# Seven-product MLP sums kept in PSUM by bank-to-bank copies, residual rows parked in DRAM

## The chip, the cores and the metric

The kernel runs on one core of one Trainium2 chip. The metric is the device time of one execution in microseconds (us). The median of three runs before the change is 256.88 us (256.54 to 257.63). One execution of the same program was also taken by the hardware profiler. It is the source of every line quoted here.

The engines have their usual short names. PE is the matrix engine; PEld is its weight load. DVE is the vector engine, ACT the scalar engine, POOL the GpSimd engine, SP the sync engine. PE writes only PSUM, eight banks of 128 partitions by 512 float32. ACT and DVE read PSUM and write either memory. DMA queues are fed from POOL and from SP.

## The reference, cut to what matters

```
P = sort_net; five times: softmax over rows, then divide by column sums      (4, 8, 8, 8)
k_sorted, v_sorted = P applied to the 8 blocks of 96 tokens of k and v
attn = softmax(0.125 * q_block @ k_sorted_block^T) @ v_sorted_block          per block
x = attn, heads side by side                                                 (4, 768, 512)
u = x + real(FFT over tokens and channels of x)
un = (u - mean(u)) / sqrt(var(u) + 1e-6)                                     over channels
out = u + relu(un @ w_ch1) @ w_ch2              w_ch1 (512, 2048), w_ch2 (2048, 512)
```

There are 4 batches (b = 0 to 3) of 768 tokens, 8 heads of 64 channels, float32 in and out. The kernel computes matrix products in float16 with float32 sums.

## The kernel before, in words

**Tiles.** A batch is 6 tiles of 128 tokens (T = 0 to 5), in two groups g = 0 and 1 of three tiles (384 tokens). For T = 0 to 2 the rows of a tile are stored with plain DMAs from SP; for T = 3 to 5 the rows are in reversed token order and are written with an indirect DMA from POOL that takes the row numbers from the tile `rows`.

**Stages of a batch.** `kqt` mixes k with the sort matrix and transposes q; `scores` makes the products and exponentials; `av` makes the 8 products with v and a division; `dft1` and `dft2` make the Fourier part and leave u (tile `u`, a pool of six buffers; batch 2 has six others, `ux`), its mean and variance, the normalised rows `un` and their transpose `ut`. Then come the MLP's two products, `ff1` (hidden rows in `hr`) and `ff2`.

**The MLP.** Batch 0 uses plain products (`ff1`, `mlp`): for each of 16 hidden chunks and each group, 4 matmuls of 128x128 by 384 (L1558), one relu out of PSUM, then `ff2` with 16 matmuls of 512 columns (L1615) and one DVE sum with u (L1622).

From batch 1 on, `ff2` is a two by two block product done with seven block products instead of eight (Winograd's form of Strassen's method). The blocks are two groups of tokens, two halves of the hidden rows and two halves of the output. The weight sums T1, T2, T4 and t3 are made once (`w2_sums`); the sums of the hidden rows (S1, S2, S3, S4) are made per chunk by DVE (L1770). A chunk (`ff2_chunk`) is tile t of both groups. Its seven products (L1794, 8 matmuls of 256 columns each) go to four PSUM banks R1, Q, R6 and R7. The sums of products that the method needs are made by DVE, reading a bank and a tile in SBUF and writing SBUF (L1811, seven instructions per chunk), after one ACT copy of R1 (L1825). The sums end in u0 and u1, the residual tiles, and `store` writes these.

`ff1` uses seven products for batches 2 and 3 alone (`SEVEN = (2, 3)`, `ff1_seven`, L1694). A `pair(i)` is one of eight hidden chunk pairs: seven products of two matmuls of 384 columns in three banks A, D, Q. A is copied three times to SBUF by ACT while it grows (`snap`, L1714). DVE adds a copy to D or Q (L1702) and makes the relu in SBUF (L1708); one relu is made by ACT out of PSUM (L1732). The weight sums G1 to G4 are made once (`w1_sums`), with one of them written over a half of w1; the sums of normalised rows (E1, E2, E4) per batch by DVE (L1682).

**Order.** Nothing is scheduled at run time. Each operation is added to a `Plan` with the engines that may do it. Five lists written out in the source (`ORDER`) give the operations of PE, ACT, DVE, POOL and SP in the order in which each engine runs them, and so also which of ACT and DVE does an operation that both may do. The plan places tiles and PSUM banks in buffers by its own running estimate of times, and fills PE's early waits with dummy matmuls (L1973). The engines wait for each other by semaphores, each strictly in its list's order.

**Memory that is reused.** `kq` has eight slots of k and q: batch 0 and 2 use slots 0 to 3, batch 3 uses 4 to 7. T1, T2, T4 lie over slots 0 to 3, G1, G2, G4 over 4 to 7.

Of the kernel before, what the change touches and what calls it, by code (L numbers as in the profile page):

```python
# [32 lines left out]
SEVEN = (2, 3)  # L33
ORDER = {
# [32 lines left out]
    ),  # L67
    "ACT": (
# [1937 lines left out]
```

## Time and profile before

| | before |
|---|---|
| median of three runs | 256.88 us |
| span of the profiled execution, first to last instruction | 254.8 us |
| PE busy | 245.2 us |
| DVE busy | 234.2 us |
| ACT busy | 165.3 us |
| POOL busy | 57.5 us |
| mean granted TensorE clock | 0.997 |
| DMA from POOL / from SP | 18.35 MB / 7.71 MB |

The profiled execution's own time is not reported beside its span. The median of the runs is 2.1 us above the span, and this document takes these 2.1 us for what lies around the span. "Busy" is the time in which at least one instruction of the engine was under way. Instructions on one engine overlap by some tens of nanoseconds, so that an engine that shows as fully busy may still take more work. Idle time of an engine that nobody waits for costs nothing. In the tables of groups, a row has the source line, the engine, the operation, what it writes and reads, the shape, the count, then total busy us and mean ns of one.

### The profile page before, as it was taken

To read this page: it belongs to the slowest core of one execution; us is meant where nothing else is said; L and a number is where in the kernel's file an instruction comes from. 1 tells how busy PE (TensorE), PEld (TensorE's weight loads), DVE (VectorE), ACT (ScalarE), POOL (GpSimd) and SP (SyncE) were. 2 spreads that over 40 slices of the span, in tenths; PEclk is the share of its full clock that TensorE was granted. 3 is DMA by queue.
4 is the path that set the end of the run, shared out by engine and by line. 5 is a ranking of instruction groups with operands and counts; after the bars stand their busy time and mean duration, and the time that the engine had idled before them with its cause. 6 is when DMAs were issued, how large, how long until landed. Compare 5 with 4: busy or idle time off the path is not lost.

```text
span 254.8 us, 7461 instructions
## 1 busy us (share of the span) xinstructions
PE 245.2 (96%) x2996; PEld 167.0 (66%) x2996; DVE 234.2 (92%) x597; ACT 165.3 (65%) x376; POOL 57.5 (23%) x88
## 2 busy tenths in 40 slices
PE   4999999999999999999999999999999999999992
PEld 1347875566566676644667757888657887567882
DVE  4799998999999989978999998999999999999993
ACT  2599998999968879956797377622687323773000
POOL 8974532234400770003100000210100000050013
PEclk9999999999999999999999999999999999999998
DMA  6999999999942699524132002530202400220025
GB/s 134 202 215 300 210 217 214 208 211 187 150 49 75 86 193 120 64 43 136 44 38 44 1 8 46 98 125 35 82 3 41 84 3 0 85 88 37 3 82 207
DMA packets 42809, 26.54 MB, mean 104 GB/s; under 512 B 30234, under 2 KB 39208, under 8 KB 42772
## 3 DMA queue, kind: packets, MB, share of 16 engines
q0 software_dynamic: 23664, 18.35, 42.9%
q1 hardware_dynamic: 19110, 7.71, 15.0%
q8 instruction: 23, 0.38, 0.6%
q14 instruction: 12, 0.10, 0.1%
HBM read 29.07 MB, written 6.29 MB: 139 GB/s over the span
## 4 chain that ended last, share of the span: by engine, by line
PE 71%; issue 9%; DVE 9%; ACT 8%; POOL 2%; DMA 1%; POOLq 0%; DVEq 0%
PE bank L1558 15%; PE bank L1794 14%; PE bank L1694 12%; PE bank L1615 9%; PE bank L1275 4%; PE bank L1440 3%; PE bank L945 2%; PE bank L1236 2%; ACT vcx L855 2%; PE bank L1349 2%; POOL out_dram L1593 2%; DVE rt L1292 1%; PE bank L1444 1%; PE bank L1047 1%; PE bank L1140 1%
## 5 line engine op out<-in xcount | busy, mean ns | idle before, releaser
L1558 PE MATMUL bank<-ut,w1sb 128*128 128x384 f16 x256 | 48.2, 326 | 0.0
L1714 ACT COPY vsf<-bank 128x384 f32<-128x384 f32 x48 | 21.6, 482 | 24.0 <-PE bank L1694 23.6
L1245 ACT ACTIVATE ex<-bank 96x384 f32<-96x384 f32 x64 | 29.3, 487 | 7.6 <-PE bank L1236 6.2
L1558 PEld LDWEIGHTS <-w1sb 128*128 128x128 f16 x256 | 23.1, 98 | 14.1 <-issue 0.3
L1570 ACT ACTIVATE hr<-bank 128x384 f16<-128x384 f32 x56 | 26.3, 491 | 8.5 <-PE bank L1558 8.5
L1593 POOL DMA_INDIRECT out_dram<-u,rows x9 | 9.4, 1042 | 97.4 <-DVE u L1811 72.5
L1794 PEld LDWEIGHTS <-hr 128*128 128x128 f16 x288 | 28.2, 98 | 4.6
L1702 DVE TENSOR_TENSOR hr<-bank,vsf 128x384 f16<-128x384 f32 x48 | 25.2, 548 | 1.6 <-PE bank L1694 1.0
L1615 PE MATMUL bank<-w2sb,hr 128*128 128x512 f16 x96 | 23.6, 380 | 0.0
L1794 PEld LDWEIGHTS <-vcx 128*128 128x128 f16 x216 | 21.1, 98 | 3.2
L1694 PE MATMUL bank<-ut,w1sb 128*128 128x384 f16 x96 | 20.7, 326 | 0.0
L1794 PE MATMUL bank<-w2sb,hr 128*128 128x256 f16 x144 | 18.7, 272 | 0.0
L1275 PEld LDWEIGHTS <-eb 97*128 97x128 f16 x416 | 15.7, 98 | 3.1 <-issue 0.4
L1794 PE MATMUL bank<-kq,vcx 128*128 128x256 f16 x144 | 17.5, 272 | 0.0
L1694 PEld LDWEIGHTS <-w1sb 128*128 128x128 f16 x128 | 12.5, 98 | 7.5
L612 POOL DMA_DIRECT2D kq<-in_q_dram x18 | 15.4, 866 | 8.8 <-PE bank L1558 4.2
L1292 DVE TENSOR_TENSOR rt<-bank,rz 128x384 f16<-128x384 f32 x32 | 16.9, 547 | 0.2
L1275 PE MATMUL bank<-vsf,eb 97*128 97x65 f16 x416 | 16.9, 193 | 0.0
L855 ACT CAST ks<-bank 128x384 f16<-128x384 f32 x27 | 14.4, 555 | 3.1 <-PE bank L1140 3.0
L1260 ACT ACTIVATE eb<-ex,negone 96x384 f16<-96x384 f32 x26 | 15.9, 616 | 0.1
L855 ACT CAST vsf<-bank 96x512 f16<-96x512 f32 x22 | 14.2, 679 | 1.4 <-PE bank L945 1.4
L1258 DVE TENSOR_SCALAR eb<-ex 96x384 f16<-96x384 f32 x38 | 13.9, 371 | 0.6 <-ACT ex L1245 0.4
(195 smaller groups left out, 535.5 us busy)
## 6 DMA issues: line engine op xcount, KB each, us to landing
w1sb<-in_moe_w_ch_dram POOLq DMA_DIRECT2D x4, 512.0 KB, 18.6
w2sb<-in_moe_w_ch_dram POOLq DMA_DIRECT2D x4, 512.0 KB, 21.5
hr<-in_v_dram POOLq DMA_DIRECT2D x2, 768.0 KB, 8.8
kq<-in_v_dram POOLq DMA_DIRECT2D x2, 768.0 KB, 12.7
kq<-in_k_dram POOLq DMA_DIRECT2D x8, 192.0 KB, 6.5
kq<-in_q_dram POOLq DMA_DIRECT2D x16, 96.0 KB, 6.7
out_dram<-u SPq DMA_DIRECT2D x5, 256.0 KB
kq<-in_k_dram POOLq DMA_DIRECT2D x2, 384.0 KB, 11.7
```

The lines of the kernel that those rows point to most:

```text
L855: (nc.scalar.copy if e == "ACT" else V.tensor_copy)(dst, src)
L1245: nc.scalar.activation(ex.ap[0:96], pss[h2].ap[0:96, 0:384], AF.Exp, scale=SCALE),
L1260: nc.scalar.activation(ed, src, AF.Identity, bias=negone[0:96])
L1275: nc.tensor.matmul(po.ap[:, 65 * T:65 * T + 65], eb.ap[:, e0:e0 + 128], vsf[0:97, vi:vi + 65], start=(n == 0), stop=(n == len(WIN[T]) - 1) ...
L1292: P.add({"DVE": (0.465, 0.56)}, lambda _: V.tensor_tensor(rt.ap[:, :, D * h:D * h + D], po3()[:, :, 0:D], rz.ap[:, :, None].broadcast_to([ ...
L1558: nc.tensor.matmul(ps.ap[:, 0:GT], w1sb[:, c, 128 * fc:128 * fc + 128], ut.ap[:, c, :], start=(c == 0), stop=(c == 3))
L1570: nc.scalar.activation(hr[g][:, fc, :], ps.ap[:, 0:GT], AF.Relu)
L1615: nc.tensor.matmul(ps.ap, hr[g][:, fc, 128 * tt:128 * tt + 128], w2sb[:, fc, :], start=(fc == 0), stop=(fc == 15))
L1694: nc.tensor.matmul(ps.ap[:, 0:GT], lhs[:, c, fi], rhs()[:, c, :], start=(start and c == 0), stop=(c == 1), skip_group_check=True)
L1702: return P.add({"DVE": (0.47, 0.57)}, lambda _: V.tensor_tensor(hr[g][:, fc, :], p.ap[:, 0:GT], o.ap, op=ALU.add), r=r, w=hk(g, fc, fc + 1 ...
L1714: P.add({"ACT": act(GT)}, lambda _: nc.scalar.copy(x.ap, A.ap[:, 0:GT]), r=[A], w=[x], prio=pr_v - 1, tag="pc", after=avs)
L1794: nc.tensor.matmul(ps.ap[:, o:o + 256], lhs()[:, fc], rhs[:, fc], start=(start and fc == 0), stop=(fc == 7), skip_group_check=True)
```

## The change

1. `SEVEN` becomes (1, 2, 3): batch 1's first product is divided into seven as well. Its sums E and its copies use tiles of the pool `s`.
2. In `ff1_seven` a pair has two banks A and Q instead of three. Sums of products are made by copying one bank over another (`seed`, PSUM to PSUM, by ACT or DVE) and letting the next matmuls accumulate on the copy. One product (G3 with B12) is copied to SBUF; DVE adds it twice.
3. `ff2_chunk` does the same with two banks and two seeds per chunk. The MLP's result no longer goes into u but into a tile z of its own, by copies (ACT or DVE) for the left group's halves and by one DVE sum each for the other two halves.
4. u is written to the output by DMA as soon as it exists (`park`), and z is added to it in DRAM by a DMA with an adding write, issued from POOL (`addup`). The last chunk of batch 3 (t = 1) still adds in SBUF and stores once.
5. T1, T2, T4 now lie over `kq` slots 4 to 7 and G1, G2, G4 over 0 to 3. `rows` has a fourth column per batch.
6. All five lists of `ORDER` are new.

```diff
-SEVEN = (2, 3)
+SEVEN = (1, 2, 3)
 ORDER = {
...
-            u = Buf("ux" if b == 2 else "u")
+            u = Buf("u")
...
+            if (b, tt) != (3, 1):
+                park(b, 3 * g + tt, u, pv)
...
+    def by_rows(b, T, t_, op):
+        i = 4 * b + T - 2
+        nc.gpsimd.memset(between, 0.0)
+        return nc.gpsimd.indirect_dma_start(
+            out.rearrange("b s m -> (b s) m"),
+            bass.IndirectOffsetOnAxis(ap=rows[:, i:i + 1], axis=0),
+            t_, None, compute_op=op)
...
+    def addup(b, T, z, pr_v):
+        def f(_):
+            if T < 2:
+                t0 = TOK[T][0]
+                nc.gpsimd.memset(between, 0.0)
+                x = nc.gpsimd.dma_start(out[b, t0:t0 + 128, :], z.ap,
+                                        accum_op=ALU.add)
+            else:
+                x = by_rows(b, T, z.ap, ALU.add)
+            unordered([x], "POOL", parked[b, T])
...
-            P.add({"DVE": (0.6, 0.69)}, lambda _, u=u, ps=ps:
-                  V.tensor_tensor(u.ap, ps.ap, u.ap, op=ALU.add),
-                  r=[ps, u], w=[(u, 1)], prio=pr_v, tag="res")
-            store(b, 3 * g + tt, u, pr_v)
+            P.add({"ACT": act(512), "DVE": (0.6, 0.69)},
+                  lambda e, z=z, ps=ps: copy(e, z.ap, ps.ap),
+                  r=[ps], w=[(z, 0), (z, 1)], prio=pr_v, tag="pc")
+            addup(b, 3 * g + tt, z, pr_v)
...
+    def seed(n, dst, src, pr_v):
+        P.add({"ACT": act(n), "DVE": dve(n)}, lambda x: copy(
+            x, dst.ap[:, 0:n], src.ap[:, 0:n]), r=[src], w=[dst],
+            prio=pr_v - 1, tag="seed")
...
+            prod(Q, G3, B12, w1k + [(ub, "d")], True)
+            P.add({"ACT": act(GT)}, lambda _: nc.scalar.copy(
+                x_(), Q.ap[:, 0:GT]), r=[Q], w=[x3],
+                prio=pr_v - 1, tag="pc", after=vmixed if early else avs)
+            prod(A, X11, B11, w1k + ak, True)
+            seed(GT, Q, A, pr_v)
+            prod(Q, X12, B21, w1k + ak, False)
+            relu(0, i, Q)
             prod(A, G2, e_(E2), ["g2", E2], False)
+            seed(GT, Q, A, pr_v)
             prod(A, X22, e_(E4), w1k + [E4], False)
+            add(0, i + 8, A)
+            prod(Q, G1, e_(E1), ["g1", E1], False)
+            add(1, i + 8, Q)
             prod(Q, G4, B22, ["g4"] + bk_, False)
+            relu(1, i, Q)
...
+        prod(Q, h_(1, 0), t3, hkk(1, 0, 0, 8) + [("ws", 1)], True)
+        P.add({"ACT": act(256)}, lambda _: nc.scalar.copy(
+            x3.ap[:, 0:256], Q.ap[:, 0:256]), r=[Q], w=[x3], prio=pr_v,
+            tag="pc")
...
+        prod(A, h_(0, 0), W11, hkk(0, 0, 0, 8) + lo8, True)
+        seed(256, Q, A, pr_v)
+        prod(Q, h_(0, 1), W21, hkk(0, 1, 0, 8) + hi8, False)
+        out_(z0, 0, Q, "l" if final else 0)
...
+        prods(A, S2, T2, [("ws", 2)])
+        seed(256, Q, A, pr_v)
+        prod(A, h_(1, 1), T4, hkk(1, 1, 0, 8) + [("ws", 3)], False)
+        out_(z1, 0, A, 1 if final else 0, x3)
+        prods(Q, S1, T1, [("ws", 0)])
+        out_(z1, 1, Q, 1, x3)
+        if final:
+            park(b, 3 + t, u1, pr_v)
         else:
+            addup(b, 3 + t, z1, pr_v)
+        prods(Q, S4, W22, hi8)
+        out_(z0, 1, Q, 1)
...
```

More of the change, by code (lines that the diff above doesn't have):

```diff
@@ L1573, in ff1, with unordered, park @@
                   w=hk(g, fc, fc + 1), prio=pr_v, tag="relu")
-    def store(b, T, u, pr_v, half=None):
+    def unordered(ins, eng, but=()):
+        for x in ins:
+            for y, of in stores:
+                if y not in but and "POOL" in (eng, of):
+                    tc.declare_no_dep(x.ins, y.ins,
+                                      reason="each row written by its own two")
+        stores.extend((x, eng) for x in ins)
+    def by_rows(b, T, t_, op):
[5 more added lines that the diff above has]
+            t_, None, compute_op=op)
+    def park(b, T, u, pr_v, half=None):
         def f(_):
@@ L1590, in f @@
             else:
[L1591 to L1601 removed]
+                st_ = [by_rows(b, T, u.ap, ALU.bypass)]
+            parked.setdefault((b, T), []).extend(st_)
+            unordered(st_, "SP" if T < 3 else "POOL")
         P.add({"SP": (0.58 if T < 2 else 1.4, 4.0 if b < 3 else 2.7)}
@@ L1637, in w2_sums @@
     def w2_sums(pr):
-        free = users(["tab"] + [x for n in range(4) for x in kqk(n)])
+        free = users(["tab"] + [x for n in range(4, 8) for x in kqk(n)])
         for n, (d, x, y, r) in enumerate((
@@ L1652, in w1_sums @@
     def w1_sums(pr):
-        free = users([x for n in range(4, 8) for x in kqk(n)])
+        free = users([x for n in range(4) for x in kqk(n)])
         w1k = [("w1", c) for c in range(4)]
@@ L1711, in relu @@
                     tag="relu")
-            def snap():
-                x = Buf("vx")
-                P.add({"ACT": act(GT)}, lambda _: nc.scalar.copy(
-                    x.ap, A.ap[:, 0:GT]), r=[A], w=[x], prio=pr_v - 1, tag="pc",
-                    after=avs)
-                return x
-            gate = ends[max(i - 2, 0):i - 1] if i > 1 else ()
-            prod(A, X11, B11, w1k + ak, True, gate)
-            prod(D, X12, B21, w1k + ak, True, gate)
-            x = snap()
-            add(0, i, D, x, [D, x])
@@ L1786, in ff2_chunk, with prod @@
                  hkk(0, 1, lo, hi) + [(S2, lo)], [(S4, lo)])
-        pools = ("pm", "pf") if b > 1 else ("pm",)
-        R1, Q, R6, R7 = (Buf(*pools) for _ in range(4))
-        def prod(ps, o, lhs, rhs, r, start, w, after=()):
+        A, Q, x3 = Buf("pm", "pf"), Buf("pm", "pf"), Buf("ex")
+        free = ("u", "ux") if b > 1 else ("u",)
+        z0, z1 = (u0, u1) if final else (Buf(*free), Buf(*free))
+        def prod(ps, lhs, rhs, r, start):
             def f(_):
@@ L1801, in h_, with prods, f @@
+        def prods(ps, S, rhs, r):
+            def f(_):
+                for fc in range(8):
+                    nc.tensor.matmul(
+                        ps.ap[:, 0:256], S.ap[:, fc], rhs[:, fc],
+                        start=False, stop=(fc == 7), skip_group_check=True)
+            P.add(pe(mm(256, 8), 8), f,
+                  r=[(S, lo) for lo, _ in parts] + r, w=[ps],
+                  prio=pr_pe + 10.1, tag="ff2")
         def h_(g, n):
-            return lambda: hr[g][:, 8 * n:8 * n + 8, tc_]
```

209 lines of the change are left out of this document (81 added, 128 removed), and 208 rows, old and new, of the table ORDER.

## The prediction

> **What bounds the kernel now.** I read the page first (shares, slices), then the busy time in stretches of 10 us, the chain of waits, the groups by line, and last the timeline of the final 15 us.
>
> ```profile
> span 254.8 us, 7461 instructions
> PE 245.2 (96%) x2996; PEld 167.0 (66%) x2996; DVE 234.2 (92%) x597; ACT 165.3 (65%) x376; POOL 57.5 (23%) x88
> PEclk9999999999999999999999999999999999999998
> ```
>
> ```profile
> core 0: us, PE busy (x) PEld busy (x) DVE busy (x) ACT busy (x) POOL busy (x), PEclk, DMA share, GB/s
> ...
> 70.00:80.00 10.00, 10.00 (x184) 6.57 (x183) 9.99 (x17) 6.91 (x15) 0.00 (x0) 1.00 0.41 58
> ...
> 130.00:140.00 10.00, 10.00 (x174) 6.71 (x171) 9.70 (x31) 7.79 (x21) 0.00 (x0) 1.00 0.30 43
> ...
> 200.00:210.00 10.00, 10.00 (x92) 8.76 (x91) 9.84 (x23) 2.11 (x5) 0.00 (x0) 1.00 0.17 34
> ```
>
> ```profile
> 18.29 0.49 PE bank L999 x2
> ...
> 38.79 0.69 DVE fo L1330 x2
> ...
> 41.41 0.70 DVE bdk L832
> 42.25 0.38 PE bank L1140 x24
> ...
> 42.94 0.44 PE bank L1440 x4
> 43.38 0.22 PE bank L1444
> ...
> 51.04 0.68 DVE u L1467
> ...
> 61.49 0.40 PE bank L1275 x13
> ...
> 64.07 0.46 PE bank L1236 x32
> 64.53 0.76 PE bank L1558 x4
> ...
> 71.48 0.51 PE bank L1140 x48
> ...
> 74.62 0.65 PE bank L1558 x4
> ...
> 184.98 10.40 PE bank L1694 x64
> 195.38 7.86 PE bank L1794 x72
> ```
>
> Busy shares alone name two suspects, PE and DVE. The chain separates them. Until the row at 41.41 it runs through DVE and ACT; 24 matmuls of L1140 wait for a DVE tile. From about 60 us on it is PE, piece after piece. At 184.98, 64 matmuls of 384 columns follow each other in 10.40 us, 162.5 ns each; at 195.38, 72 of 256 columns in 7.86 us, 109 ns each. The clock row is full, so these are PE's own pitches and PE has no holes there. DVE's 9.84 of 10 us is softer than it looks: two sums of line 1330 take 0.69 us together, though one alone lasts 418 ns (row below). Instructions overlap by 0.07 us or more, so DVE's 597 instructions hide some 40 us of room. So: DVE and ACT set the time up to about 50 us, PE's amount of work from there to the last matmul, DMAs after it.
>
> **The change part by part.**
>
> *Batch 1's first product in seven.* Sixteen hidden chunks by two groups by 4 matmuls are 128; eight pairs by seven products by 2 are 112. PE does 16 matmuls of 384 columns fewer: 16 x 162.5 ns = 2.60 us. All other products keep their number; a chunk of the second product has 7 x 8 matmuls before and after. This term is **-2.6 us**, if PE stays full.
>
> *What DVE and ACT gain and lose.* Counts are from the two programs' instruction lists, durations from these rows:
>
> ```profile
> L1330 DVE TENSOR_TENSOR fo<-eo 128x512 f16<-128x512 f16 x8 | 3.3, 418 | 0.0
> L1811 DVE TENSOR_TENSOR u<-bank,u 128x256 f32<-128x256 f32 (+1 forms) x18 | 8.9, 503 | 0.7 <-PE bank L1794 0.6
> L1811 DVE TENSOR_TENSOR ex<-bank,ex 128x256 f32<-128x256 f32 x18 | 7.4, 418 | 1.0 <-PE bank L1794 0.7
> L1811 DVE TENSOR_TENSOR u<-u,ex 128x256 f32<-128x256 f32 (+1 forms) x12 | 6.5, 554 | 0.0
> L1811 DVE TENSOR_TENSOR eb<-bank,eb 128x256 f32<-128x256 f32 (+1 forms) x9 | 4.4, 503 | 0.0
> L1811 DVE TENSOR_TENSOR eb<-eb,ex 128x256 f32<-128x256 f32 (+1 forms) x6 | 3.3, 550 | 0.0
> L1622 DVE TENSOR_TENSOR u<-bank,u 128x512 f32<-128x512 f32 x6 | 4.1, 687 | 1.6 <-PE bank L1615 1.6
> L1567 DVE TENSOR_SCALAR hr<-bank 128x384 f16<-128x384 f32 x8 | 4.3, 545 | 0.0
> L1682 DVE TENSOR_TENSOR qt<-ut,qt 128x768 f16<-128x768 f16 x4 | 2.2, 547 | 0.0
> L1714 ACT COPY vsf<-bank 128x384 f32<-128x384 f32 x48 | 21.6, 482 | 24.0 <-PE bank L1694 23.6
> L1825 ACT COPY ex<-bank 128x256 f32<-128x256 f32 x9 | 3.4, 372 | 15.6 <-PE bank L1794 15.6
> ```
>
> DVE loses the five groups of L1811 and L1622: 30.5 + 4.1 = 34.6 us, 69 instructions. It gets 20 sums of 256 columns (418 ns, 8.4 us) and one of 512 (0.7); 16 bank-to-bank copies, half of 384 and half of 256 columns (8 x 545 + 8 x 418 = 7.7 us); 11 copies of results (5 us); four more sums E (2.2) and six more relus out of PSUM (3.3). Three PSUM copies move to ACT, some 2 us. Net about -9 us. ACT gets 50 bank-to-bank copies (40 x 482 + 10 x 372 = 23 us) and 8 result copies (4), loses 24 copies of L1714 (11.6) and six relus (3): about +14 us. No row shows a copy that writes PSUM; I price it like a copy out of PSUM, its nearest row. Both engines stay under the span, and after 60 us PE covers them. I put this at **0** here; its cost without that cover is the next two items and a rival. The weight sums only change their places and slots.
>
> *The start.* Ahead of the first MLP product (L1558, at 50.96 us before) the new lists put 136 DVE instructions in place of 128; the differing ones come to 2.0 us at the means of their groups. PE's list has five more other products ahead: one each of L1275 (0.40), L1236 (16 matmuls, 0.23), L1140 (24, 0.26), a q transpose (taken like L1140) and two fp32 matmuls of L999 (0.49): 1.64 us. PE thus starts the MLP about 2.0 us later with 1.64 us more behind it: **+0.3 us**, between -1.0 (early waits shrink, as u tiles come free after their store rather than after the MLP) and +2.0 (nothing of PE's extra work fits).
>
> *The middle.* Moving batch 1's sums forward moves attention forward too: at the last L1275 product PE has 13 first-product and 3 second-product steps fewer ahead of it and two Fourier tiles more (13 x 0.65 + 3 x 0.87 - 2 x 0.66, the last from L1440 and L1444, = 9.7 us less), while DVE still needs 303 instructions instead of 312, about 5 us less, and ACT as many as before. Between 60 and 130 us DVE and ACT therefore have 5 and 10 us less lead. The stretch 70 to 80 shows DVE at 9.99; how much lead it has no row says. I take **+0.3 us**, 0 to +3.
>
> *Changes of tile shape.* The row at 64.53, four matmuls right after small-tile ones, took 0.76 us; the same four took 0.65 at 74.62. PE's new list changes between small and full tiles 73 times, not 78: 5 x 0.11 = 0.55 us, part of it in the early waits. **-0.3 us.**
>
> *Parked rows and adding DMAs.* Twenty-two adding DMAs join POOL's queue, and the plain stores of u move forward on SP and POOL. POOL has 77% free time. Behind the first of them stands one load of k for batch 3. Three indirect stores of batch 0 stand among the loads of k and q for batch 2 and one of w2 and wait for u, which DVE made at 51.04 before; those loads come 1 to 4 us later, ahead of products of the middle, whose upper end covers them. On SP, the transposes of `un` and the row transfers stand behind early stores; SP's list is no longer than before. **0** until the end. There it differs:
>
> ```profile
> 247.31 0.96 POOL L1593 DMA_INDIRECT out_dram<-u,rows  x1 [18.46 <-DVE u L1811]
> 248.57 0.96 POOL L1593 DMA_INDIRECT out_dram<-u,rows  x1 [0.19 <-DVE ex L1811]
> 249.23 1.04 PE L1794 MATMUL bank<-w2sb,vcx 128*128 128x256 f16 x8
> 249.84 0.96 POOL L1593 DMA_INDIRECT out_dram<-u,rows  x1 [0.19 <-DVE u L1811]
> 250.30 0.42 DVE L1811 TENSOR_TENSOR u<-bank,u 128x256 f32<-128x256 f32 x1 [0.34 <-PE bank L1794]
> ```
>
> ```profile
> L1593 POOL DMA_INDIRECT out_dram<-u,rows x9: 959/963/1491, 114.8 to 249.8; - x9
> DMA to landing us min/median/max: 2.7/2.9/3.8
> ```
>
> PE ends at E = 250.27, and the last POOL store begins 0.43 us earlier, lands about 2.9 us after its issue, and the span ends 4.5 us after E. POOL issues 1.26 us apart. In the new list the last five of POOL are: add, add, add, add, store, where before stood three stores. Counted back from E in products of 0.87 us, the fourth add waits for a copy of the product that ends at E - 1.7, and the store for a sum of the one that ends at E - 0.9, ready at E - 0.35. With 0.85 us per plain and 1.26 per indirect issue, the adds keep POOL until about E, and the store begins near E + 0.3 instead of E - 0.4. **+0.8 us**, from 0 (POOL not late) to +1.3 (all five 1.26 apart), if the adds move their bytes as fast as the stores do.
>
> *The sum.* -2.6 + 0.3 + 0.3 - 0.3 + 0.8 = -1.5 us. The span goes from 254.8 to 253.3, and with the 2.1 us around it the time is **255.4 us** against the median of 256.88. Its own range is 253.8 to 257.2: the distances of the terms to their ends, as roots of summed squares (below 1.3, 0.3, 0.25, 0.8: 1.6; above 1.7, 0.3, 0.5: 1.8), with the middle's upper end left to its rival. Half a per cent, 1.3 us, is about what a measurement of this kernel can tell from no change.
>
> **The rivals.**
>
> *More gain than PE's work.* The start's lower end, another 1.3 us, together with a tail that does not grow (0.8): 255.4 - 2.1 = 253.3, and 253.0 with the middle at 0. For it: u tiles freed early let `dft2` of later batches run when it likes. Against: the lists put more, not less, DVE work ahead of the first MLP product.
>
> *Seeds stop PE (the other side).* PE is in order; a product that accumulates on a copied bank waits for the copy. Of the 66 copies, by PE's list and the pitches above, 17 have under 1.0 us of other products between the product copied and the one that needs the copy. A copy takes 0.48 us, and a matmul's result comes 0.16 us after its pitch (busy 326 ns, row below, against 162.5): 0.7 us with the waits. With 0.25 us lost at each of the 17, PE ends 4.2 us later: 259.6. It decides from 0.09 us per copy on, where the 1.5 us are gone. For it: ACT, which makes 50 of the copies, is busy 6.91 and 7.79 of 10 us in the stretches from 70 and 130, and a copy that queues is late. Against: 2.11 in the stretch from 200, and the shortest cover is 0.83 us.
>
> ```profile
> L1694 PE MATMUL bank<-ut,w1sb 128*128 128x384 f16 x96 | 20.7, 326 | 0.0
> ```
>
> *Adding DMAs are slow.* An add reads and writes 256 KB in DRAM. No row shows one. If each holds the queue 2 us instead of less than 1.26, the four before the last store delay it by 3 us: 258.4.
>
> *DVE and ACT bind from 60 to 130 us.* The middle's upper part, +1.8 rather than +0.3, gives 257.2 with a hole in PE near 70 to 85 us.
>
> *POOL's issues are held by DVE.* Of nine indirect issues one took 1491 ns, the median 963. If all five at the end took the longest, they would add 5 x 0.53 = 2.6 us: 258.0. Eight of nine rows speak against it, three of them in the tail itself at 0.96 with DVE full. The Trainium skill, "SBUF — State Buffer", section "Who interferes with whom", says that GpSimd and DVE share a port pair and that a DVE copy or scalar operation in a two-port mode blocks GpSimd's descriptor writing; by that rule the tail is safe, as its DVE work is two-input sums and copies out of PSUM, and the 0.96 us rows agree.
>
> **How the numbers follow.** The forecast 0.45, more gain 0.18, seeds 0.12, slow adds 0.12, the middle 0.10, held issues 0.03. Faster by over 0.5% (under 255.6): 0.28 of the forecast and all of more gain, 0.46. Within: 0.17 of the forecast, 0.06 of the middle, 0.01 of held issues, 0.24. Slower (over 258.2): the rest, 0.30. The range reaches from 1.2 us below more gain's 253.0 to a little over the seeds' 259.6: 251.8 to 260.0.
>
> **What would show it.** PE's work: 3 x 112 = 336 matmuls in the seven-product line, 128 in the plain one, at the pitch of 162.5 ns. Seeds: DVE and ACT copies bank to bank near 0.48 us, and in the last 100 us no idle time of PE that ends with a copy. DVE near 225 us busy, ACT near 180. Tail: PE's end 4.5 + 0.8 us ahead of the end of the span; issue to landing of an adding DMA near 3 us. The prediction is wrong if PE waits on a bank copy for more than 1 us in sum, if the first MLP product starts after 54 us, or if an adding DMA needs over 5 us to land.

## The result and the profile after

The changed kernel takes 273.63 us (median of four runs, 271.73 to 275.2) against 257.01 us for the kernel before on the same chip. The ratio is 1.065 [1.060, 1.070]: it is slower by 16.6 us. 255.4 us was forecast, and the range ended at 260.0. One execution of e3_plain_writes (268.38 us) was in a slower state; it is in that kernel's median and not in its ratio.

The page of the changed kernel, its shares and one of its groups:

```profile
span 273.3 us, 7516 instructions
PE 245.8 (90%) x2974; PEld 165.6 (61%) x2974; DVE 224.9 (82%) x581; ACT 180.5 (66%) x413; POOL 89.8 (33%) x132
...
L859 ACT COPY bank<-bank 128x384 f32<-128x384 f32 (+1 forms) x50 | 22.1, 450 | 16.2 <-PE bank L1852 4.3
```

DVE's and ACT's busy times came out as priced. PE is busy for about as long as before, but on a span 18.5 us longer. Its holes lie in four places. The first is at the start (timeline, first instructions of SP's loads, then of PE):

```profile
1.28 0.71 POOL L616 DMA_DIRECT2D hr<-in_v_dram  x1 [0.83 <-POOLq L2003]
...
2.03 0.34 SPq L616 DMA_DIRECT2D pack<-k_pack  x1
...
9.75 4.48 PE L1986 MATMUL bank<-pack 128*128 128x480 f16 x13 [9.75 <-DMA pack<-k_pack]
...
59.03 1.47 PE L1563 MATMUL bank<-ut,w1sb 128*128 128x384 f16 x8
```

The same places in the kernel before:

```profile
1.20 0.41 SPq L612 DMA_DIRECT2D pack<-k_pack  x1
1.27 1.32 POOL L612 DMA_DIRECT2D hr<-in_v_dram  x2 [0.82 <-POOLq L1990]
...
3.71 4.46 PE L1973 MATMUL bank<-pack 128*128 128x480 f16 x12 [3.71 <-DMA pack<-k_pack]
...
50.96 1.47 PE L1558 MATMUL bank<-ut,w1sb 128*128 128x384 f16 x8
```

The tile `pack` (tables that many early matmuls read) was the second load on SP's list and is now the fourth. Its issue moves by 0.8 us, from just ahead of POOL's 768 KB load of v to behind it, and its data arrive 6 us later. The first MLP product starts 8.1 us later. What stands between is partly padding: the 13 matmuls at 9.75 are dummies (L1986) whose number is fixed in the program. They too read `pack`, and PE's first needed product (L877) comes behind them:

```profile
14.07 1.46 PE L877 MATMUL bank<-hr,pack 128*128 128x512 f16 x6
```

In the kernel before that product (L873) started at 8.66, when the first load of v had landed.

The other three places show in the busy time of 10 us stretches of the changed kernel (columns as in the prediction; the last four are POOL's busy time, the granted clock, the DMA share and GB/s):

```profile
110.00:120.00 10.00, 8.39 (x187) 5.34 (x186) 8.89 (x26) 7.97 (x18) 3.42 (x5) 1.00 0.63 133
120.00:130.00 10.00, 8.80 (x119) 4.48 (x121) 5.75 (x16) 7.19 (x17) 0.85 (x2) 0.83 0.22 65
...
180.00:190.00 10.00, 9.10 (x69) 6.49 (x67) 6.61 (x14) 3.79 (x9) 4.04 (x8) 1.00 0.75 107
190.00:200.00 10.00, 9.06 (x56) 5.39 (x56) 9.24 (x28) 6.79 (x18) 1.72 (x2) 1.00 0.26 52
...
260.00:270.00 10.00, 3.45 (x31) 2.69 (x28) 1.87 (x4) 0.58 (x2) 5.82 (x9) 0.79 0.89 144
```

Between 110 and 130 PE has holes and, behind them, a granted clock under 1. Between 180 and 200 it has smaller ones. From 264.5 on only DMAs work. The tail of the changed kernel (timeline, POOL and the last matmuls):

```profile
258.79 1.56 POOL L1591 DMA_INDIRECT out_dram<-u,rows  x1 [15.73 <-DVE u L1870]
260.66 1.56 POOL L1591 DMA_INDIRECT out_dram<-u,rows  x1 [0.19 <-issue]
262.53 1.56 POOL L1591 DMA_INDIRECT out_dram<-eb,rows  x1 [0.19 <-issue]
262.93 1.03 PE L1852 MATMUL bank<-w2sb,vcx 128*128 128x256 f16 x8 [0.52 <-DVE u L1870]
...
263.53 1.54 POOL L1630 DMA_DIRECT2D out_dram<-eb  x1
...
265.37 1.02 POOL L1591 DMA_INDIRECT out_dram<-u,rows  x1 [0.19 <-issue]
```

PE ends at 263.96, and the span 9.3 us later; before it was 4.5 us. Three adding issues 1.87 us apart, and a fourth behind them, hold back the one plain store that is last, which begins 1.4 us after PE's end.

### The profile page after: what moved, and what is told of

Read it like the earlier page. It is cut to its first block, busy times and chain, and to the rows that moved or that the text cites. A ratio compares the mean times of both kernels' runs of the same rounds, so it can differ in the third digit from the quotient of the medians.

```text
span 273.3 us, 7516 instructions
## 1 busy us (share of the span) xinstructions
PE 245.8 (90%) x2974; PEld 165.6 (61%) x2974; DVE 224.9 (82%) x581; ACT 180.5 (66%) x413; POOL 89.8 (33%) x132
## 5 line engine op out<-in xcount | busy, mean ns | idle before, releaser
L1591 POOL DMA_INDIRECT out_dram<-u,rows x22 | 28.5, 1296 | 109.2 <-DVE u L1870 40.2
L1742 PE MATMUL bank<-ut,w1sb 128*128 128x384 f16 x144 | 31.9, 326 | 1.3 <-DVE u L1479 0.8
L859 ACT COPY bank<-bank 128x384 f32<-128x384 f32 (+1 forms) x50 | 22.1, 450 | 16.2 <-PE bank L1852 4.3
L1742 PEld LDWEIGHTS <-w1sb 128*128 128x128 f16 x192 | 18.7, 98 | 13.4 <-issue 2.2
L1563 PE MATMUL bank<-ut,w1sb 128*128 128x384 f16 x128 | 25.0, 326 | 0.9 <-issue 0.6
L1646 PE MATMUL bank<-w2sb,hr 128*128 128x512 f16 x96 | 25.3, 389 | 0.0
L1765 ACT ACTIVATE hr<-bank 128x384 f16<-128x384 f32 x40 | 19.1, 493 | 7.8 <-PE bank L1742 7.4
L1742 PEld LDWEIGHTS <-kq 128*128 128x128 f16 x144 | 14.0, 98 | 9.7 <-issue 0.5
L1750 DVE TENSOR_TENSOR hr<-bank,vsf 128x384 f16<-128x384 f32 x32 | 17.0, 547 | 3.0 <-PE bank L1742 2.6
L859 ACT CAST vsf<-bank 96x512 f16<-96x512 f32 x25 | 16.1, 680 | 1.1 <-PE bank L949 1.1
L1264 ACT ACTIVATE eb<-ex,negone 96x384 f16<-96x384 f32 x27 | 16.6, 622 | 0.2
L1986 PE MATMUL bank<-pack 128*128 128x480 f16 x26 | 8.0, 445 | 9.8 <-DMA pack<-k_pack 9.8
L1563 PEld LDWEIGHTS <-w1sb 128*128 128x128 f16 x128 | 11.3, 97 | 8.3 <-issue 1.7
```

The costliest lines, as they stand in the source:

```text
L859: (nc.scalar.copy if e == "ACT" else V.tensor_copy)(dst, src)
L1563: nc.tensor.matmul(ps.ap[:, 0:GT], w1sb[:, c, 128 * fc:128 * fc + 128], ut.ap[:, c, :], start=(c == 0), stop=(c == 3))
L1591: return nc.gpsimd.indirect_dma_start(out.rearrange("b s m -> (b s) m"), bass.IndirectOffsetOnAxis(ap=rows[:, i:i + 1], axis=0), t_, None, ...
L1646: nc.tensor.matmul(ps.ap, hr[g][:, fc, 128 * tt:128 * tt + 128], w2sb[:, fc, :], start=(fc == 0), stop=(fc == 15))
L1742: nc.tensor.matmul(ps.ap[:, 0:GT], lhs[:, c, fi], rhs()[:, c, :], start=(start and c == 0), stop=(c == 1), skip_group_check=True)
L1750: P.add({"DVE": (0.47, 0.57)}, lambda _: V.tensor_tensor(hr[g][:, fc, :], p.ap[:, 0:GT], x_(), op=ALU.add), r=[p, x3], w=hk(g, fc, fc + 1) ...
```

## The experiments

A label in each heading names the kernel. Each ratio is to the kernel before, run on the same chip.

### The place of one load: e1_pack_second, e2_before_pack_fourth

The first is the changed kernel with `pack` second on SP's list again, the second the kernel before with `pack` fourth and the loads around it as in the changed list.

```diff
-        "12 17 16 13 14 15 230 231 232 233 279 428 ..."
+        "12 13 17 16 14 15 230 231 232 233 279 428 ..."
```

```diff
-        "12 13 14 15 233 231 17 232 230 16 421 ..."
+        "12 17 16 13 14 15 233 231 232 230 421 ..."
```

> The changed kernel with one move: the load of pack goes back from the fourth to the second place of SP's list, ahead of rows and rrow. Theory start: pack leaves after the first v load has been issued (2.03 us against 1.28) and its packets stand behind that load's 1.5 MB; first of all it lands at 9.75 us instead of 4.48, PE's list, which is in order, begins with matmuls that read it, and everything up to the first MLP product moves by 5 us. Then pack lands near 4.5 us, the first product of line 1563 starts near 54 us instead of 59.0, and the time falls by 4 to 5 us, from 273.6 to about 269. Rival: the early delay is absorbed, since PE had slack behind the loads of w1 and the waits for DVE until 60 us: then pack lands early and the time stays within 1 us of 273.6.

> The kernel before with the same one move in the other direction: pack fourth on SP's list, behind rows and rrow, nothing else. Theory start: pack lands near 9.8 us instead of 4.48, the first MLP product starts about 5 us later than 51.0, and the time rises by 4 to 5 us to about 261.5. Rival, the delay is absorbed: 257 to 258.

Measured: 269.02 us, ratio 1.045 [1.042, 1.049], and 266.28 us, 1.035 [1.032, 1.038]. So the place of `pack` costs the changed kernel 273.63 - 269.02 = 4.6 us and would cost the kernel before 8.9 us, twice what was expected of it. The timelines, first of the changed kernel with `pack` second, then of the kernel before with `pack` fourth:

```profile
3.65 4.98 PE L1986 MATMUL bank<-pack 128*128 128x480 f16 x12 [3.65 <-DMA pack<-k_pack]
...
54.51 1.47 PE L1563 MATMUL bank<-ut,w1sb 128*128 128x384 f16 x8
```

```profile
10.33 9.76 PE L1973 MATMUL bank<-pack 128*128 128x480 f16 x39 [10.33 <-DMA pack<-k_pack]
...
60.16 1.47 PE L1558 MATMUL bank<-ut,w1sb 128*128 128x384 f16 x8
```

The first product of the MLP follows the arrival of `pack`: 4.5 us earlier in the one, 9.2 us later in the other. Much of the 8.9 us is padding: the second kernel has 50 dummy matmuls instead of 32, 39 of them in one row behind `pack`, and its first needed product starts at 19.92 instead of 8.66. No run leaves the dummies out, so what the late load alone costs stays open.

That `pack` waited for the load of v and not for the two small loads ahead of it on SP's list shows in `rows`, one of these two. By the semaphore steps it landed at 2.8 us in the changed kernel, where it was issued at 1.20, ahead of v, and at 8.3 us in e1_pack_second, where it was issued at 1.65, behind v. The first load of v landed at 8.5 and 8.1 us. (The expectation's 4.48 us for the landing of `pack` in the kernel before is a misreading; it is 3.71.)

12 us of the 16.6 are left.

### The adding writes: e3_plain_writes, e4_no_adds

Both start from e1_pack_second. The first writes z with plain DMAs in the same places, the second issues no DMA for z at all.

```diff
-                x = nc.gpsimd.dma_start(out[b, t0:t0 + 128, :], z.ap,
-                                        accum_op=ALU.add)
+                x = nc.gpsimd.dma_start(out[b, t0:t0 + 128, :], z.ap)
...
-                x = by_rows(b, T, z.ap, ALU.add)
+                x = by_rows(b, T, z.ap, ALU.bypass)
```

```diff
-            if T < 2:
...
-            unordered([x], "POOL", parked[b, T])
+            nc.gpsimd.tensor_copy(between, z.ap[:, 0:512:512])
```

> As the run with pack second, and the 22 adding DMAs write their rows without adding: same bytes out of SBUF, same queue, same waits. It leaves out the residual term of the rows so written: the parked rows are overwritten. Theory adding mode: an add costs POOL 1.56 us to issue and holds the queue longer than a plain write because DRAM is read too; plain writes issue in 0.96 us (indirect), the u buffers come free in 3 us instead of 4.5 to 8, the hole of PE between 183 and 197 us (3.5 us of idle time) goes, and the tail from PE's end to the span's end falls from 9.4 to about 5.5 us: together 6 to 7 us less than with pack second alone. Rival, number of transfers: the 22 more writes of 256 KB do this whatever their mode; then no more than 2 us are won.

> As the run with pack second, and no adding DMA is issued at all: in its place POOL copies one column of the MLP's result tile, so that the waits of POOL and the release of the tile stay. It leaves out the MLP term of all rows but the last tile pair's. If the adding mode is the cause, this is as fast as the plain writes within 1.5 us; if the number of writes is, it is faster than the plain writes by over 3 us. The hole of PE between 106 and 126 us (6.5 us more idle time than before) tells its cause as well: if it is unchanged here, the adds are not behind it, and seed copies or the parked rows are; if it goes, the adds are.

Measured: 265.77 us, 1.031 [1.027, 1.035], and 260.13 us, 1.009 [1.006, 1.013]. Without any DMA for z, 269.02 - 260.13 = 8.9 us go. Plain writes instead of adding ones bring 3.7 us of these (by the ratios, 0.0145 x 257), not the 6 to 7 us expected. By the forecast's own terms a kernel without adds stands at -1.5 - 0.8 = -2.3 us, 255 us on this chip (257.34 before). 260.13 us is 5 us more, with no wait in PE's list that is long enough to explain it.

In the trace they showed as matmuls whose result was ready and whose reader did not start. One place, in e1_pack_second (the last column is the idle time before the instruction, and what ended it):

```profile
106.95 0.36 PE L1144 MATMUL bank<-bdk,kq 64*64 64x64 f16 x24
107.23 1.61 POOL L1591 DMA_INDIRECT out_dram<-u,rows  x1 [4.13 <-ACT u L859]
...
108.71 0.58 ACT L859 CAST ks<-bank 128x384 f16<-128x384 f32 x1 [1.25 <-PE bank L1563]
108.82 0.58 DVE L859 CAST ks<-bank 128x384 f16<-128x384 f32 x1 [1.10 <-PE bank L1563]
...
109.35 0.84 PE L1279 MATMUL bank<-vsf,eb 97*128 97x65 f16 x22 [1.28 <-ACT ks L859]
```

The 24 transposes end at 107.31. The copies of their result wait until 108.7, and PE then waits 1.28 us for a copy. In between lies an indirect DMA's issue on POOL, which has no part in these data. An engine tells the others that an instruction is done by a step of its semaphore, the signal. For every PE, DVE and ACT instruction of a trace that gives one I worked out the time from its recorded end to the next step of its engine's semaphore. In the changed kernel 47 of 1291 such signals came over 0.5 us late, the latest 2.74 us. All 47 instructions ended within 1.5 us of the start of an indirect issue on POOL, where 312 of the 1291 ended. Several steps come together: the four late signals of PE from 51.19 to 51.76 in e1_pack_second all step at 52.45, 1.38 us behind the start of an issue.

This measure has a limit. In 32 of the 47 cases the step found is also that of a later instruction of the same engine, so that a late signal can't be told there from a step that the trace lacks. The readers decide: at 9 moments another engine had been idle for 0.3 to 2.2 us and started its next instruction within 0.15 us of the late step.

An issue is counted below when an instruction that ended in the 1.3 us behind its start has a late signal. These are 17 of the 27 indirect issues of the changed kernel, 16 of the 27 of e1_pack_second, 9 of the 12 of e4_no_adds and 1 of the 12 of the kernel before. They are 17 of 27 in e3_plain_writes, so the adding mode is not needed for it, and 5 of 12 in e2_before_pack_fourth, the kernel before with one load moved. There PE waits for nothing over 0.3 us once `pack` has landed, and needs 204.2 us from the first MLP product to the span's end, against 203.8 before, so the late signals cost at most 0.4 us there.

### Direct transfers only: e5_direct, e6_before_direct, e7_direct_no_adds, e8_direct_plain

All indirect DMAs become direct ones of the same size, in the changed kernel with `pack` second (e5), in the kernel before (e6), in e4_no_adds (e7), and in e5 with plain writes for the adds (e8).

```diff
-        i = 4 * b + T - 2
+        lo, n = (257, 127) if T == 2 else (min(TOK[T]), 128)
         nc.gpsimd.memset(between, 0.0)
-        return nc.gpsimd.indirect_dma_start(
-            out.rearrange("b s m -> (b s) m"),
-            bass.IndirectOffsetOnAxis(ap=rows[:, i:i + 1], axis=0),
-            t_, None, compute_op=op)
+        kw = {} if op == ALU.bypass else dict(accum_op=op)
+        return nc.gpsimd.dma_start(out[b, lo:lo + n, :], t_[0:n], **kw)
```

> As the run with pack second, with every indirect DMA on POOL (14 parks and adds of the second half's tiles in each pair, and the adds of the third tile) made a direct one of the same bytes from the same tile. It leaves out the reversal: the rows of the second half come out in ascending order of the tile, and row 0 of each batch misses its MLP term. Theory signals: while POOL issues an indirect DMA, signals of PE, DVE and ACT arrive 0.5 to 2.7 us late; in the trace with pack second nearly all signals of PE that came over 0.5 us late lie within 1.5 us of the start of one of the 28 indirect issues, and the holes of PE at 107.7 to 109.4 and 116 to 118 us begin at such an issue. Then both holes go, no signal is late by over 0.5 us, and the time falls by 3 to 5 us, from 269.0 to about 265. Rival, contention in the memory: the holes come from the DMAs' transfers, which stay; then the time moves by less than 1 us.

> The kernel before with its 9 indirect stores made direct in the same way (the rows of the second half come out in the tile's order; nothing else is left out). Theory signals: before, one of the nine issues delayed signals of PE (by 0.6 us at 114.9), and the last three stand at the end, where a direct issue takes 0.6 us instead of 0.96 and less time between them: 0.5 to 1.5 us faster than before, 255.8 to 256.8. Rival: no difference, under 0.5 us.

> As the run without adds (260.1 us), with its 12 indirect parks made direct. It leaves out the MLP term of all rows but those of the last tile pair, and the reversal. What remains is the seven-product change, the bank-to-bank copies and the new order. Theory signals: the late signals at 52.8, 62 to 64, 103, 114 to 116 and 153 us go, worth 2 to 4 us: 256 to 258. If seeds or the new order cost PE time by themselves, it stays at 259 to 260, and the trace shows PE waiting for ACT's or DVE's copies at other places.

> As the run with all POOL transfers direct (262.1 us), and the 22 adds become plain writes of the same bytes. It leaves out the residual of the rows so written, and the reversal. With the run without adds (256.0 us) it splits what the adds still cost when no indirect issue is left. Theory adding mode: a transfer that adds lands 5 to 8 us after its issue and a plain one after some 3; then the wait of DVE for a u tile near 175 us (2.1 us) and the long tail (7.7 us from PE's end to the span's end) both go, and the time is 256 to 257.5. Rival, number of transfers: 22 more writes of 256 KB cost the same in either mode: 260 to 262.

| `pack` second, and | with indirect DMAs | with direct ones alone |
|---|---|---|
| adding writes | 269.02, ratio 1.045 | 262.14, ratio 1.019 [1.016, 1.021] |
| plain writes | 265.77, ratio 1.031 | 257.53, ratio 1.000 [0.999, 1.002] |
| no DMA for z | 260.13, ratio 1.009 | 255.95, ratio 0.996 [0.994, 0.997] |
| the kernel before | 1 | 256.34, ratio 0.997 [0.996, 0.999] |

None of the four kernels with direct DMAs alone has a single late signal (the largest is under 0.1 us), and the kernel before gains almost nothing from direct ones. By the ratios, times 257 us, the adding mode costs 0.0185 x 257 = 4.8 us where all DMAs are direct, and 22 more plain writes cost 0.0048 x 257 = 1.2 us (e8 ran on another chip than e5 and e7). With indirect DMAs, 3.7 us of the 8.9 went with the mode and 5.2 with the writes. But e3 has 27 indirect issues, 17 with late signals, and e4 has 12, 9 with late signals, so this pair changes two things. The landing times of the adds to the first tiles (their line's view), in e5_direct and then in e8_direct_plain; the columns are the issue's duration in ns, least, median and most:

```profile
L1628 POOL DMA_DIRECT2D out_dram<-u x4: 852/908/1177, 85.3 to 170.7; - x4
...
DMA to landing us min/median/max: 4.1/6.9/8.4
```

```profile
L1628 POOL DMA_DIRECT2D out_dram<-u x4: 540/551/574, 87.1 to 172.0; - x4
...
DMA to landing us min/median/max: 2.3/2.8/6.1
```

With the same 256 KB from the same place, an adding DMA takes 0.91 us to issue instead of 0.55, and 6.9 us to land instead of 2.8.

### What makes a signal late: e9_before_12_indirect, e10_before_12_direct, e11_scratch_256, e12_scratch_1504, e13_scratch_direct

The question was whether an indirect issue always delays the signals beside it. e9 adds twelve indirect DMAs of 256 B rows to the kernel before, behind loads on POOL between 53 and 95 us; e10 adds direct ones in the same places. e11 and e12 add twelve indirect ones to e7_direct_no_adds, of 256 B and of 1504 B rows, behind each park on POOL; e13 adds direct ones of 1504 B.

```diff
+                scr = nc.dram_tensor(f"scr{i}", (B * S, 64), F32,
+                                     kind="Internal").ap()
+                nc.gpsimd.memset(between, 0.0)
+                nc.gpsimd.indirect_dma_start(
+                    scr, bass.IndirectOffsetOnAxis(
+                        ap=rows[:, i:i + 1], axis=0), pack[:, 0:64], None)
```

> The kernel before with 12 more indirect DMAs: on POOL, behind every second load of k, q and w2 issued from about 37 to 95 us, a memset of one column and an indirect DMA of 128 rows of 256 bytes from pack to a scratch tensor that nothing reads. Theory signals: each holds the signals of PE, DVE and ACT for about 1.3 us from its start, in the stretch where PE waits for both often. The trace shows late signals at these places, and the time rises by 2 to 6 us over the same kernel with direct DMAs. Rival: an indirect issue costs POOL's own time alone, some 0.4 us more than a direct one; POOL has room there, and both kernels take the same time within 0.7 us.

> The control: the same 12 additions to the kernel before with direct DMAs of the same bytes. Both theories: 257 to 258.5, no late signals at these places; the additions take POOL some 0.7 us each and delay the loads behind them.

> As the run without adds and with direct parks (256.0 us; leaves out the MLP term of all rows but the last tile pair's, and the reversal); behind each of its 12 direct parks on POOL comes an indirect DMA of 128 rows of 256 bytes from pack to a scratch tensor that nothing reads. Theory place: the holds depend on where in the program the issue stands, so they are back: signals late by over 0.5 us at most of the 12, and 258.5 to 260. Theory transfer (2-KB rows, a tile just written): no signal late by over 0.5 us or few, and 256 to 257.

> The same with rows of 1504 bytes (192 KB for each of the 12). Theory place: as with 256-byte rows. Theory size: 259 to 260 here and 256 to 257 there. Theory of the tile just written, or of the wait that the issue itself carries: both stay at 256 to 257.5.

> Control: the 12 transfers of 1504-byte rows from pack as direct DMAs. All theories: no late signals, 256 to 257.

| | us | ratio | indirect issues, with a late signal |
|---|---|---|---|
| e9_before_12_indirect | 257.84 | 1.001 [1.000, 1.002] | 24, 3 |
| e10_before_12_direct | 257.84 | 1.001 [0.999, 1.002] | 12, 1 |
| e11_scratch_256 | 259.49 | 1.009 [1.007, 1.011] | 12, 6 |
| e12_scratch_1504 | 261.6 | 1.015 [1.013, 1.018] | 12, 8 |
| e13_scratch_direct | 257.13 | 1.001 [0.999, 1.002] | 0, 0 |

Twelve indirect DMAs that nobody waits for cost 2.4 and 4.5 us against the direct ones of e13, in a kernel whose direct twin is undisturbed, so an indirect issue alone can bring the loss. (The trace of e12 is of its fastest execution, 258.34 us, so its 8 don't stand for the median.) But twelve more in the kernel before cost nothing, not the 2 to 6 us expected, with late signals beside 3 of 24 issues. The size of the rows doesn't settle it, 6 and 8 of 12. Whether the kernel or the execution decides was open.

### The same programs again: e14_before_again, e15_before_12_again, e16_scratch_256_again, e17_no_adds_again, e18_pack_second_again

Unchanged copies, on other chips: the kernel before, e9, e11, e4 and e1.

> The kernel before, profiled a second time. If the program fixes which indirect issues delay signals: again 1 of 12, at 114.8 us. If each execution draws: another count, or other places.

> The kernel before with 12 more indirect issues, a second profile. Program: again 3 of 24, at 53.3, 89.5 and 95.2 us. Execution: another count or other places.

> The changed kernel without adds, with direct parks and 12 indirect issues of 256-byte rows behind them, a second profile. Program: again 6 of 12, at 52.7, 63.3, 112.3, 114.2, 150.4 and 152.3 us. Execution: another count or other places.

> The run without adds, with its 12 indirect parks (leaves out the MLP term of all rows but the last tile pair's), a second time. If the delay belongs to the program after all: 9 of 12 issues delay a signal and 260.1 us. If it is drawn by the execution or the chip: another count, and with few late signals 256.5 to 258.

> The run with pack second, a second time. Program: 16 of 27 issues delay a signal and 269.0 us. Execution or chip: with few late signals 263 to 266 us, as the longer issues and landings of the adds stay (262.1 us with direct transfers).

| same program | first: us, issues with late signals | again: us, issues with late signals |
|---|---|---|
| before / e14 | 257.01, 1 of 12 | 257.25, 1 of 12 |
| e9 / e15 | 257.84, 3 of 24 | 257.19, 2 of 24 |
| e11 / e16 | 259.49, 6 of 12 | 257.86, 0 of 12 |
| e4 / e17 | 260.13, 9 of 12 | 256.75, 0 of 12 |
| e1 / e18 | 269.02, 16 of 27 | 265.47, 1 of 27 |

e14 to e16 are single times, beside a single 256.77 us of the kernel before. e17 has the ratio 0.999 [0.996, 1.001] and e18 1.032 [1.027, 1.037]. So the program alone does not decide how many signals are late, and the same two programs took 3.4 and 3.5 us more where many were. The counts go with the chip as far as the runs reach: e1 to e4 shared one chip, e11 and e12 another, and on the three chips of the other experiments with indirect issues at most 3 of 24 are counted. No run separates the chip from the single execution.

Where a signal is late is partly fixed by the program. e14 has its one at 114.8 us again, as the first reading of its expectation had it; e10 and e15 have one at the same transposes, at 115.2 and 115.1 us. The changed kernel, e1 and e4 have the same four late signals of PE at their first indirect issue, the longest of them 1.22 to 1.26 us.

The place shown above, in e18_pack_second_again:

```profile
105.13 0.36 PE L1144 MATMUL bank<-bdk,kq 64*64 64x64 f16 x24
105.26 1.61 POOL L1591 DMA_INDIRECT out_dram<-u,rows  x1 [3.42 <-ACT u L859]
...
105.95 0.59 ACT L859 CAST ks<-bank 128x384 f16<-128x384 f32 x1 [0.47 <-PE bank L1144]
106.07 0.58 DVE L859 CAST ks<-bank 128x384 f16<-128x384 f32 x1 [0.17 <-PE bank L1144]
...
106.59 0.96 PE L1279 MATMUL bank<-vsf,eb 97*128 97x65 f16 x26 [0.35 <-ACT ks L859]
```

The same issue of 1.61 us stands beside the same transposes, and the copies begin 0.46 us after the transposes' end instead of 1.40 us. From 100 to 120 us PE is busy for 19.65 us in this trace and for 17.10 us in that of e1_pack_second, which holds 2.55 of the 3.5 us.

This pair, e17 without adds and e18 with them, is also where the adds can be priced with next to no late signals: 265.47 - 256.75 = 8.7 us. Their profiled spans are 255.8 and 263.3 us. Two places hold the difference. The stretches of e17_no_adds_again, then those of e18_pack_second_again with the rows of its timeline in them:

```profile
170.00:180.00 10.00, 10.00 (x79) 7.51 (x77) 8.51 (x19) 3.21 (x8) 0.18 (x1) 1.00 0.01 2
180.00:190.00 10.00, 10.00 (x66) 6.26 (x65) 9.94 (x29) 8.71 (x22) 0.00 (x0) 1.00 0.07 26
```

```profile
170.00:180.00 10.00, 9.06 (x66) 6.22 (x64) 6.83 (x15) 3.83 (x9) 3.63 (x6) 1.00 0.74 107
180.00:190.00 10.00, 9.09 (x57) 5.45 (x57) 9.05 (x26) 7.08 (x17) 1.72 (x2) 1.00 0.29 52
```

```profile
176.38 0.69 DVE L1470 SCALAR_TENSOR_TENSOR u<-rt,bank 128x510 f32<-128x510 f16 x1 [2.47 <-DMA out_dram<-u,rows]
...
179.41 0.49 PE L1742 MATMUL bank<-ut,w1sb 128*128 128x384 f16 x2 [0.77 <-DVE u L1479]
...
180.33 1.03 PE L1852 MATMUL bank<-w2sb,vcx 128*128 128x256 f16 x8 [0.44 <-DVE u L1870]
...
252.44 1.03 PE L1852 MATMUL bank<-w2sb,vcx 128*128 128x256 f16 x8 [0.51 <-DVE u L1870]
...
254.88 1.02 POOL L1591 DMA_INDIRECT out_dram<-u,rows  x1 [0.19 <-issue]
```

From 170 to 190 PE loses 20.0 - 18.15 = 1.85 us. DVE's next u has no free buffer, since z takes its tiles from the pool of u, and a DMA that reads one of them has not landed; PE's waits for DVE follow. The rest is the tail: PE ends at 253.47 and the span 9.8 us later, against 251.74 and 4.1 us without adds, 5.8 us more. With direct DMAs alone the adds cost 262.14 - 255.95 = 6.2 us, so 2.5 of the 8.7 us go with their being indirect.

## Why the prediction was wrong

The steps from the change without adds to the result, each a difference of two medians. Neighbouring rows share a median, so the column adds up by construction, and the runs are from several chips:

| | us |
|---|---|
| the change, `pack` second, no adds, no late signals (e17) | 256.75 |
| the adds (e18 - e17; on another chip e1 - e4 gives 8.9) | +8.7 |
| late signals (e1 - e18; e4 - e17 gives 3.4) | +3.5 |
| `pack` fourth (after - e1) | +4.6 |
| after | 273.6 |

The first row holds -2.6 us of work and the waits that used it up. The row of `pack` also holds whatever the 47 late signals of the changed kernel cost more than the 35 of e1; the 4.5 us by which the first MLP product moved stand beside its 4.6.

**Batch 1's first product in seven** (-2.6 us) was right as work. The lines of the seven products hold 336 matmuls and the plain line 128, 16 fewer in all. **Changes of tile shape** (-0.3) are too small for any run to tell apart.

**What DVE and ACT gain and lose** was right: 224.9 and 180.5 us busy, against 225 and 180. Copies from bank to bank, for which there was no row, take 450 ns on ACT and 491 on DVE, against 480.

**The rival "Seeds stop PE"** did not come. PE's waits in the changed kernel:

```profile
PE bank L1852 <- DVE u L1870: 1.0, 2, 0.5
...
PE bank L1742 <- DVE bank L859: 0.2, 1, 0.2
```

One copy from bank to bank kept PE waiting, 0.2 us in all. The two waits of 0.5 us are for sums that still read a bank.

**The start** (+0.3 us, up to +2.0) failed, and its largest part is an edit that the prediction did not look at. It counted DVE's and PE's lists ahead of the first MLP product and not SP's, where `pack` had moved by two places: 4.6 us. "About 2.0 us later" was 8.1 us, and the sign that it named, a first MLP product after 54 us, is there at 59.03. With `pack` second it is 3.0 us (53.97 in e18_pack_second_again) to 4.1 us (55.09 in e17_no_adds_again). Less the 1.64 us of PE's work that moved ahead of it, the term is +1.4 to +2.5 us, about at its upper end. One wait of PE in e17_no_adds_again is in none of the rows of before:

```profile
PE bank L921 <- DVE vcx L989: 1.6, 1, 1.6
```

Which move in the new lists makes it, no run separates.

**The middle** (+0.3 us, up to +3) was too small but inside its range. From the first MLP product to its last matmul PE needs 251.74 - 55.09 = 196.7 us in e17, and 250.27 - 50.96 = 199.3 before: 2.7 us less. By the forecast's terms it would be 2.6 + 1.64 - 0.3 + 0.3 = 4.2 us less, so the middle is about +1.9 us. That is the size of the rival **"DVE and ACT bind"**, but the hole that it named is not there: PE is busy for all of 70 to 90 us. Start, middle and work together leave e17 at 0.999 of before, where the forecast without its tail term was -2.3 us: the 2.6 us of work were gained and lost again to waits that PE had not had. (The profiled execution of e17 took 257.91 us, 1.2 us above its median, so these terms are rather too large.)

**"Parked rows and adding DMAs"** (0 until the end, then +0.8, at most +1.3) is the step that failed most: 8.7 us. The add was priced like a store. Four sizes were off. The indirect adding issues take 1.56 us and stand 1.87 us apart, not 1.26. The direct ones take 0.90 to 1.56 us, in the tail 1.54. The last store begins 1.4 us after PE's end instead of 0.3. And the adds ahead of it hold the data: the span ends 7.9 us after the start of that last issue, 5.0 us before. The tail is 9.3 us long instead of the 5.3 forecast. The other part was "0 until the end": z tiles hold the buffers of u until slow DMAs land, and DVE waits for one (the 2.47 us above). The rival **"Adding DMAs are slow"** had this mechanism, with 3 us for the tail and nothing for the buffers. The sign that it named, more than 5 us to land, is there: a median of 6.5 us in e18_pack_second_again, line L1630.

**The rival "POOL's issues are held by DVE"** had the right symptom, issues of 1.5 us, and a wrong cause: without the adding mode the median indirect issue takes 0.963 us in e3_plain_writes beside the same DVE work.

**Late signals** (3.5 us) were in no step. The trace of before shows one, which the prediction did not look for, and no row of it foretells 17 issues with late signals. What makes them late stays open. The Trainium skill, "SBUF — State Buffer", section "Who interferes with whom", says that PE and ACT never wait on anyone and that DMAs do not contend with the engines; the 31 late signals of PE and ACT in the changed kernel, beside indirect issues, are not covered by it, though what is late here is the signal and not the engine's access to memory.

No version beats the kernel before. The two that are a little faster, e6 and e7, leave out work that the reference needs.

## What to carry to other kernels

When all the lists of a kernel are new, compare the first loads of every queue, by what they stand next to: 0.8 us in the order of issue cost 6 us of arrival. Padding that reads a late load moves with it. An addition moved from an engine into a DMA is not free because the queue's engine is idle; price its issue, its landing, and the buffers that it keeps until then, above all at the end where nothing covers it. Where a trace shows an engine starting long after its input's producer ended, look at what else was being issued at that moment, and run the same program again elsewhere before putting it down to the program.

## What the runs showed of the hardware that was not expected

A load of `pack` that was issued 0.75 us after a load of 768 KB landed 7.7 us after its own issue (2.03 to 9.75); issued 0.07 us ahead of it, 2.5 us (1.20 to 3.71). Loads of a single row in the same stretch did not wait: those of `rrow`, `vrow` and `erow` landed within 0.5 us of their issue.

Signals of PE, DVE and ACT come up to 2.7 us late in the changed kernel beside indirect DMA issues of POOL, on some chips or in some executions, and in none of the five kernels without indirect issues. The size of the rows showed no pattern (6 and 8 of 12). What decides it stays open.

The granted clock fell after a short hole. The stretch behind the late signals of the changed kernel at 119 to 122 us:

```profile
119.00:120.00 1.00, 0.65 (x24) 0.38 (x20) 1.00 (x3) 0.19 (x1) 0.81 (x3) 1.00 0.49 124
120.00:121.00 1.00, 0.69 (x3) 0.12 (x2) 0.18 (x1) 0.00 (x0) 0.85 (x2) 1.00 0.62 209
121.00:122.00 1.00, 0.11 (x4) 0.11 (x4) 0.13 (x1) 0.65 (x2) 0.00 (x0) 1.00 0.68 236
122.00:123.00 1.00, 1.00 (x15) 0.54 (x14) 1.00 (x3) 1.00 (x3) 0.00 (x0) 0.70 0.19 60
123.00:124.00 1.00, 1.00 (x3) 0.15 (x1) 0.53 (x2) 1.00 (x4) 0.00 (x0) 0.50 0.00 0
124.00:125.00 1.00, 1.00 (x5) 0.34 (x4) 0.00 (x0) 0.64 (x3) 0.00 (x0) 0.50 0.00 0
125.00:126.00 1.00, 1.00 (x15) 0.83 (x15) 0.00 (x0) 0.81 (x3) 0.00 (x0) 0.59 0.00 0
```

PE was idle for about 1.5 of the first three microseconds, and then ran for about 4 us at 0.50 to 0.70 of its clock, which adds to what a late signal costs.
